# A chunked attention and MLP kernel: first weight quarter by tiles, weights loaded ahead of the rest of keys and queries

## The chip, the cores and the metric

One core of one Trainium2 chip. The metric is the device time of one execution in microseconds (us). All runs quoted are "fast": none lies more than 1.5% above the fastest of its kernel. The engines are called TensorE (PE in the profile, its weight loads PEld), VectorE (DVE), ScalarE (ACT), GpSimd (POOL) and SyncE (SP).

## The reference

Four batches, eight heads, 768 positions, head size 64. Each chunk of 32 queries looks at its own positions, 16 before, 8 behind and 8 memory positions. The result goes through a normalisation and a two-layer MLP of width 2048 with a residual.

```python
for c in range(S // 32):
    ctx = positions max(0, 32*c - 16) .. min(S, 32*c + 40)
    scores = q_c @ concat(mem_k, k[ctx]).T / sqrt(64)
    out_c  = softmax(scores) @ concat(mem_v, v[ctx])
x  = out as (4, 768, 512)
xn = (x - mean(x)) / sqrt(var(x) + 1e-6) * g_ln
out = x + relu(xn @ w_ch1) @ w_ch2          # 512 -> 2048 -> 512
```

## The kernel before

The 24 tiles of 128 tokens are worked off in eight units of three. A unit has 28 steps: 16 up steps (`up`, one for each 128 of the 2048 hidden values) and 12 down steps. Between them, a plan `at(step, ...)` places the attention of the next unit, the turns (transposes) of keys and queries, the clears of buffers and the loads. Unit 0 has nothing before it, so its own attention stands in a start stage, where filler matmuls (`stay_busy`) on a zero tile keep TensorE occupied.

Names in the profile lines: `kraw` and `qraw` are keys and queries as loaded, `KT` and `QZ` the same turned, `V` the values, `xs`, `xn` and `xT` a tile before the norm, after it and turned, `rT` the hidden values after relu, `w1c` and `w2c` the quarters of W1 and W2. `mm` and `att` are buffers in PSUM, where matmuls leave their results; a buffer is free again once another engine has copied it out.

```python
def up(u, n, hc):                      # one step: 4 matmuls of 384 columns, then relu
    p = slot("mm")[:, 0 : 128 * n]     # four PSUM banks "mm", taken in rotation
    for dt in range(4):
        nc.tensor.matmul(out=p, lhsT=free(w, i, [[4, 128]]), rhs=xT[u % 2][:, dt, 0 : 128 * n], ...)
    if hc % 2: nc.scalar.activation(out=o, in_=p, func=ACTF.Relu)
    else:      nc.vector.tensor_scalar(out=o, in0=p, scalar1=0.0, ..., op0=ALU.max)
# ... cut: start stage, loads by GpSimd in program order:
#     k, q rows 0-63 | V groups 0-5 | W1 quarters 0-2 | k, q rows 64-95 | W1 quarter 3 | W2 0, 1 | ...
    def attend(steps, kind="dma"):
        for i, (s0, s1, s2, s3) in enumerate(steps):
            t = following[i]
            at(s0, scores, t // 6, t % 6)
            at(s1, values, t // 6, t % 6)
            at(s2, norm, t % 6, t % 9)             # VectorE
            at(s3, turn_x, u + 1, i, t % 6, kind)  # TensorE turns, ScalarE copies to xT
            at(min(s3 + 3, 27), root, t % 6, t % 9)# ScalarE squares
    if u == 0:
        at(1, clear_q, 1, 0);  at(5, clear_q, 1, 1)
        at(14, clear_k, 1);    at(16, clear_v, 1)  # VectorE memsets for batch 1
        for j in (0, 2):
            at(10 + j, kq_block, 0, j, 6, NG, "att")   # turns of the rest of k and q
            at(11 + j, keep_rest)
        # ... cut
        attend(((16, 19, 19, 22), (17, 21, 21, 24), (19, 23, 23, 26)), "att")
```

The softmax here doesn't subtract the row's maximum and nothing guards it: scores larger than these inputs give would overflow.

Of the kernel before, what the change touches and what calls it, by code (L numbers as in the profile page):

```python
# [15 lines left out]
def kernel(  # L16
# [12 lines left out]
    nc = tc.nc  # L29
# [3 lines left out]
    NG = 12  # L33
    KR = 96
    HD = 80
    CUT = 64

    ctx.enter_context(tc.manual_schedule())
    sb = ctx.enter_context(tc.tile_pool(name="sb", bufs=1))
# [44 lines left out]
    def slot(kind):  # L84
        lst = {"att": att, "mm": mm}[kind]
        turn[kind] = (turn[kind] + 1) % len(lst)
        return lst[turn[kind]]
# [53 lines left out]
    def load_w1(c):  # L141
        nc.gpsimd.dma_start(
            out=w1c[c], in_=dram(moe_w_ch1, 512 * c, [[FF, 128], [128 * FF, 4], [1, 512]])
        )
# [221 lines left out]



    def up(u, n, hc):
        p = slot("mm")[:, 0 : 128 * n]  # L370
        c, i = hc // 4, hc % 4
        for dt in range(4):
            w = w1c[c][:, dt, :]
            nc.tensor.matmul(  # L374
                out=p, lhsT=free(w, i, [[4, 128]]), rhs=xT[u % 2][:, dt, 0 : 128 * n],
                start=(dt == 0), stop=(dt == 3),
            )
        o = rT[hc][:, 0 : 128 * n]
        if hc % 2:
            nc.scalar.activation(out=o, in_=p, func=ACTF.Relu)  # L380
        else:
            nc.vector.tensor_scalar(out=o, in0=p, scalar1=0.0, scalar2=None, op0=ALU.max)  # L382
# [71 lines left out]
    nc.vector.memset(busy, 0.0)  # L454
    nc.vector.memset(counts, 1.0)  # L455
    nc.vector.memset(ones32, 1.0)
    nc.vector.memset(memv16[:, :, :, 64:HD], 1.0)
    nc.sync.dma_start(out=memk32, in_=dram(mem_k, 0, [[64, 128], [128 * 64, 2], [1, 64]]))
    nc.sync.dma_start(out=g_one, in_=dram(moe_g_ln, 0, [[0, 1], [1, 512]]))
    nc.sync.dma_start(out=memv32, in_=dram(mem_v, 0, [[64, 8], [512, H], [1, 64]]))  # L460
    for h in (0, 4):
        for which in range(2):
            load_kq(0, which, 0, CUT, h, h + 4)
    keep(counts[:, 0:1], counts[:, 0:1], 16, 0.0)
    keep(counts[:, 1:2], counts[:, 1:2], -80, 0.0)
    make_identity(nc, identity)
# [19 lines left out]
    nc.gpsimd.tensor_tensor(out=band[:, 0:1], in0=band[:, 0:1], in1=zero2[:, 1:2], op=ALU.add)  # L486
    for g in range(4, 6):
        load_v_group(0, g)
    for c in range(3):
        load_w1(c)  # L490
    load_kq(0, 0, CUT, 96)
    load_kq(0, 1, CUT, 96)
    load_w1(3)
    load_w2(0)
    load_w2(1)
    for g in range(6, 8):
        load_v_group(0, g)
    load_w2(2)
    for g in range(8, NG):
        load_v_group(0, g)  # L500
    load_w2(3)
    nc.gpsimd.dma_start(
# [2 lines left out]
    )  # L505

    vec, act = nc.vector.tensor_copy, nc.scalar.copy
    first_k = [as16(slot("mm")[:, :]) for j in range(4)]
    first = slot("att")
    first_q = [as16(first[:, 0, :]), as16(first[:, 1, :])]  # L510
    for j in range(2):
        turn_kq(first_k[j], k16[0], j, CUT)
    for j in range(2):
        turn_kq(first_q[j], q16[0], j, CUT)
    for j in range(2):
        keep_k(first_k[j], 0, j, CUT, 0, 7)
        for par in range(2):
            keep_q(act, first_q[j], 0, j, par, CUT, 0, 6)
    spare = att[(turn["att"] + 1) % 2][:, 0, :]
    stay_busy(3, spare)  # L520
    first_q += first_k[0:2]
    for j in range(2, 4):
        turn_kq(first_k[j], k16[0], j, CUT)
    stay_busy(5, spare)
    for j in range(2, 4):
        turn_kq(first_q[j], q16[0], j, CUT)
    for j in range(2, 4):
        keep_k(first_k[j], 0, j, CUT, 0, 7, act if j == 2 else vec)
    for j in range(2, 4):
        for par in range(2):  # L530
            keep_q(act if j == 2 else vec, first_q[j], 0, j, par, CUT, 0, 6)
    nc.vector.memset(mhalf, -0.5)
    stay_busy(3, spare)
    scores(0, 0)
    scores(0, 1)
    stay_busy(2)
    pg = slot("mm")[:, :]
    nc.tensor.matmul(out=pg, lhsT=ones32, rhs=g_one, start=True, stop=True)
    nc.vector.tensor_copy(out=g_row, in_=pg)
    stay_busy(1)  # L540
    values(0, 0)
    norm(0, 0)
    scores(0, 2)
    stay_busy(1)
    values(0, 1)
    norm(1, 1)
    stay_busy(4)
    values(0, 2)
    norm(2, 2)
    stay_busy(2)  # L550
    turn_x(0, 0, 0, "mm")
    stay_busy(2)
    turn_x(0, 1, 1, "mm")
    stay_busy(5)
    turn_x(0, 2, 2, "mm")
    stay_busy(3)
    for t in range(3):
        root(t, t)


    units = [[t, t + 1, t + 2] for t in range(0, 6 * B, 3)]
    for u, tiles in enumerate(units):
        n = len(tiles)
        following = units[u + 1] if u + 1 < len(units) else []
        plan = {}

        def at(step, fn, *args):
            plan.setdefault(step, []).append((fn, args))
# [7 lines that stand above are left out]
                at(s2, norm, t % 6, t % 9)  # L576
                at(s3, turn_x, u + 1, i, t % 6, kind)
                at(min(s3 + 3, 27), root, t % 6, t % 9)

        def cross(steps, b, t0, t1, t2):  # L580

            for half in range(2):
                at(steps[half], cross_k, b, half, t0, t1)
                at(steps[2 + half], cross_q, half, t2 - 3, t2)

        def spread(step, b, t0, t1):
            for half in range(2):
                at(step + half, spread_q, b, half, t0, t1)

        if u == 0:  # L590
            at(1, clear_q, 1, 0)
            at(5, clear_q, 1, 1)
            at(14, clear_k, 1)
            at(16, clear_v, 1)
            for j in (0, 2):
                at(10 + j, kq_block, 0, j, 6, NG, "att")
                at(11 + j, keep_rest)
            for h in (0, 4):
                for which in range(2):
                    at(12, load_kq, 1, which, 0, 96, h, h + 4)  # L600
            for g in range(6):
                at(16, load_v_group, 1, g)
            attend(((16, 19, 19, 22), (17, 21, 21, 24), (19, 23, 23, 26)), "att")
            at(26, mem_cols, 1)
            at(26, v_mem, 1)
        elif u == 1:
            for j in (0, 2):
                at(5 + 3 * j, kq_block, 1, j, 0, NG, "att")
                at(7 + 3 * j, keep_rest)
            for g in range(6, NG):  # L610
                at(0, load_v_group, 1, g)
            for t in range(6):
                for which in range(2):
                    at(14, load_tokens, 2, which, t)
            attend(((16, 19, 19, 22), (17, 19, 20, 23), (21, 23, 23, 26)), "att")
        elif following:
            if u in (2, 4):
                attend(((2, 7, 7, 7), (4, 7, 8, 8), (9, 13, 13, 13)))
            else:
                attend(((9, 14, 14, 14), (11, 14, 15, 15), (16, 20, 20, 20)))  # L620
            if u == 2:
                cross((0, 0, 1, 1), 2, 0, 4, 3)
                at(8, mem_cols, 2)
                at(8, k_around, 2, 0, 4)
                for h in range(H):
                    at(8, load_v_head, 2, h)
                spread(9, 2, 0, 3)
                cross((14, 14, 15, 15), 2, 4, 6, 6)
            elif u == 3:
                at(1, v_mem, 2)  # L630
                at(1, v_around, 2)
                at(4, k_around, 2, 4, 6)
                spread(5, 2, 3, 6)
                for t in range(6):
                    for which in range(2):
                        at(24, load_tokens, 3, which, t)
            elif u == 4:
                for h in range(H):
                    at(0, load_v_head, 3, h)
                cross((14, 14, 15, 15), 3, 0, 4, 3)  # L640
                at(17, mem_cols, 3)
                at(17, v_mem, 3)
                at(17, v_around, 3)
                at(22, k_around, 3, 0, 4)
                spread(23, 3, 0, 3)
                cross((20, 21, 24, 25), 3, 4, 6, 6)
            elif u == 5:
                at(2, k_around, 3, 4, 6)
                spread(3, 3, 3, 6)
        for step in range(16 + 4 * n):  # L650
            if step < 16:
                up(u, n, step)
            else:
                i, part = divmod(step - 16, 4)
                if u == 0:
                    d = step - 16
                    i, part = divmod(d, 2) if d < 6 else (d % 3, d // 3)
                if following or i < n - 1:
                    down(tiles[i], i, part)
                elif part == 0:  # L660
                    down_last(tiles[i], i)
            for fn, args in plan.get(step, ()):
                fn(*args)
# [30 lines left out]
```

## Time and profile before

| | before |
|---|---|
| time, median of 3 runs (a fourth was timed later, beside the change) | 220.41 us (220.31 to 220.75) |
| profiled span | 218.5 us |
| TensorE busy | 97% of the span |
| first real W1 matmul | 22.60 us |
| first full step after W1's first quarter (22.60 + 16 x 0.1625) | 25.2 us |
| first matmul of unit 1 | 50.40 us |

A busy share includes the fillers; 97% is not 97% of useful work. From 22.6 us on TensorE does useful work almost without a gap (the largest up to unit 1 is 0.20 us), so a gain has to show as an earlier start of unit 1. The lines are in the prediction below.

### The profile page before, as it was taken

How to read it: one execution, taken by the hardware profiler on the slowest of the kernel's cores; microseconds unless marked ns; L12 is line 12 of the kernel's file. 1: busy time of each engine (PE TensorE's matmuls, PEld its weight loads, DVE VectorE, ACT ScalarE, POOL GpSimd, SP SyncE). 2: the span in 40 equal slices, each digit the busy share in tenths (PEclk: the TensorE clock that was granted, in tenths of full speed). 3: DMA queues.
4: the chain of work that ended last, by engine and by line, in shares of the span. 5: the costliest groups of instructions: out<-in, count | busy, mean ns of one | idle time of the engine just before them, and what ended most of it. 6: DMA issues, size and time to landing. Idle time of an engine off the chain costs nothing.

```text
span 218.5 us, 4954 instructions
## 1 busy us (share of the span) xinstructions
PE 212.8 (97%) x1975; PEld 129.2 (59%) x1975; DVE 118.7 (54%) x269; ACT 98.6 (45%) x196; POOL 105.0 (48%) x177
## 2 busy tenths in 40 slices
PE   7998999999999999999999999999999999999994
PEld 2554677556775577545764577446754676457553
DVE  6948566576764836823366339515386337534222
ACT  4464747635884766600555077202751165403200
POOL 7984435957995226986002999626174000300000
PEclk9999999999999999999999999999999999999999
DMA  4999999999999329995605799996743200330012
GB/s 74 181 146 206 208 202 170 192 204 193 178 145 150 105 91 128 163 139 178 87 2 99 106 176 156 162 183 96 174 122 99 96 0 11 88 103 21 0 48 96
DMA packets 93089, 27.20 MB, mean 124 GB/s; under 512 B 83673, under 2 KB 89561, under 8 KB 93018
## 3 DMA queue, kind: packets, MB, share of 16 engines
q0 software_dynamic: 67504, 14.23, 73.9%
q1 hardware_dynamic: 25562, 12.66, 24.7%
q8 instruction: 15, 0.25, 0.5%
q14 instruction: 8, 0.07, 0.1%
HBM read 28.48 MB, written 6.29 MB: 159 GB/s over the span
## 4 chain that ended last, share of the span: by engine, by line
PE 90%; DVE 3%; DMA 3%; ACT 1%; issue 1%; POOL 1%; DVEq 0%; POOLq 0%
PE mm L374 38%; PE mm L391 37%; PE att L288 5%; PE att L308 3%; DMA kraw<-in_k_dram 3%; PE att L178 2%; PE mm L409 2%; DVE xs L319 1%; ACT QZ L203 1%; DVE xn L328 1%; PE att L351 1%; PE mm L178 1%; PE att L365 1%; DVE QZ L203 1%; PE mm L365 0%
## 5 line engine op out<-in xcount | busy, mean ns | idle before, releaser
L374 PE MATMUL mm<-xT,w1c 128*128 128x384 f16 x512 | 88.5, 327 | 0.0
L391 PE MATMUL mm<-w2c,rT 128*128 128x512 f16 x368 | 84.2, 379 | 0.0
L374 PEld LDWEIGHTS <-w1c 128*128 128x128 f16 x512 | 56.8, 114 | 24.3 <-issue 0.3
L380 ACT ACTIVATE rT<-mm 128x384 f16<-128x384 f32 x64 | 31.2, 489 | 68.4 <-PE mm L374 46.8
L391 PEld LDWEIGHTS <-rT 128*128 128x128 f16 x368 | 34.8, 98 | 37.8
L382 DVE TENSOR_SCALAR rT<-mm 128x384 f16<-128x384 f32 x64 | 35.1, 554 | 35.9 <-PE mm L374 35.8
L398 DVE SCALAR_TENSOR_TENSOR osb<-mm,rstd,xs 128x512 f32<-128x512 f32 x23 | 17.3, 751 | 42.3 <-PE mm L391 29.9
L295 ACT ACTIVATE AT<-att,band 96x512 f16<-96x512 f32 x48 | 30.1, 678 | 10.9 <-PE att L288 10.6
L337 POOL TENSOR_SCALAR veps<-squares 128x1 f32<-128x1 f32 x24 | 4.6, 191 | 50.5 <-ACT junk L334 49.2
L116 POOL DMA_DIRECT2D V<-in_v_dram x24 | 21.5, 903 | 8.5 <-DMA w1c<-in_moe_w_ch_dram 4.3
L334 ACT ACTIVATE junk<-xs,nmean 128x512 f16<-128x512 f32 x24 | 17.3, 719 | 7.1 <-DVE nmean L325 6.7
L328 DVE SCALAR_TENSOR_TENSOR xn<-xs,nmean,g_row 128x512 f16<-128x512 f32 x24 | 18.5, 771 | 0.9
L319 DVE SCALAR_TENSOR_TENSOR xs<-att,rec 128x512 f32<-128x512 f32 x24 | 16.6, 692 | 0.8
L276 POOL COPY QZ<-kraw 64x768 f16<-64x768 f16 x16 | 14.4, 900 | 3.5 <-DMA kraw<-qraw 2.9
L203 ACT COPY QZ<-att 64x384 f16<-64x384 f16 (+1 forms) x20 | 12.0, 599 | 8.4 <-PE att L178 8.2
L288 PE MATMUL att<-QZ,KT 128*128 128x128 f16 x192 | 14.8, 219 | 0.2 <-DVE QZ L203 0.2
L288 PEld LDWEIGHTS <-KT 128*128 128x128 f16 x192 | 12.6, 98 | 4.0 <-issue 0.3
L341 POOL TENSOR_TENSOR rstd<-veps,mhalf 128x1 f32<-128x1 f32 x24 | 13.3, 552 | 2.0
L365 PE MATMUL mm<-busy 128*128 128x512 f16 x34 | 11.1, 454 | 1.2 <-DVE counts L455 1.2
L122 POOL DMA_DIRECT2D V<-in_v_dram x16 | 12.0, 807 | 0.0
L268 POOL COPY KT<-KT 128x128 f16<-128x128 f16 (+4 forms) x16 | 4.2, 293 | 15.6 <-DMA KT<-kraw 15.6
L241 POOL DMA_DIRECT2D kraw<-in_k_dram x12 | 11.4, 954 | 0.0
(68 smaller groups left out, 133.9 us busy)
## 6 DMA issues: line engine op xcount, KB each, us to landing
out_dram<-osb SPq DMA_DIRECT2D x23, 256.0 KB, 3.0
w1c<-in_moe_w_ch_dram POOLq DMA_DIRECT2D x4, 512.0 KB, 10.0
w2c<-in_moe_w_ch_dram POOLq DMA_DIRECT2D x4, 512.0 KB, 14.2
V<-in_v_dram POOLq DMA_DIRECT2D x20, 88.0 KB, 8.5
kraw<-in_k_dram POOLq DMA_DIRECT2D x12, 128.0 KB, 4.5
qraw<-in_q_dram POOLq DMA_DIRECT2D x12, 128.0 KB, 4.6
V<-in_v_dram POOLq DMA_DIRECT2D x16, 96.0 KB, 5.3
kraw<-in_k_dram POOLq DMA_DIRECT2D x3, 256.0 KB, 6.2
```

The lines of the kernel that those rows point to most:

```text
L116: nc.gpsimd.dma_start(out=V[b % 2][r : r + hi - lo, g, :, 0:64], in_=dram(v, b * H * HS + lo * D, [[64, hi - lo], [HS, H], [1, 64]]),)
L203: copy(out=free(QZ[b % 2][rows, g0, j, par, :], 0, [[512, g1 - g0], [8, 8], [1, 8]]), in_=free(pv[rows, :], 8 * g0, [[8, g1 - g0], [1, 8], ...
L288: nc.tensor.matmul(out=p[:, gg, 128 * j : 128 * j + 128], lhsT=KT[b % 2][:, (4 * g + j) * KR : (4 * g + j) * KR + 128], rhs=QZ[b % 2][:, g ...
L295: nc.scalar.activation(out=free(a, 32 * c, [[512, 2], [64, 8], [1, 32]], KR), in_=free(p, 32 * c, [[512, 2], [64, 8], [1, 32]], KR), func= ...
L319: nc.vector.scalar_tensor_tensor(out=x.rearrange("p (h d) -> p h d", h=H), in0=free(p, 0, [[128, H], [1, 64]]), scalar=1.0, in1=free(r, 0, ...
L328: nc.vector.scalar_tensor_tensor(out=xn[i], in0=x, scalar=nmean[i], in1=g_row, op0=ALU.add, op1=ALU.mult,)
L334: nc.scalar.activation(out=junk, in_=xs[xi], func=ACTF.Square, bias=nmean[i], accum_out=squares[i],)
L374: nc.tensor.matmul(out=p, lhsT=free(w, i, [[4, 128]]), rhs=xT[u % 2][:, dt, 0 : 128 * n], start=(dt == 0), stop=(dt == 3),)
L380: nc.scalar.activation(out=o, in_=p, func=ACTF.Relu)
L382: nc.vector.tensor_scalar(out=o, in0=p, scalar1=0.0, scalar2=None, op0=ALU.max)
L391: nc.tensor.matmul(out=p, lhsT=rT[hc][:, 128 * i : 128 * i + 128], rhs=w2c[hc // 4][:, hc % 4, :], start=(hc == 0), stop=(hc == 15),)
L398: nc.vector.scalar_tensor_tensor(out=o, in0=p, scalar=rstd[t % 9], in1=xs[t % 9], op0=ALU.mult, op1=ALU.add,)
```

## The change

The intent: start unit 0's up projection before its third tile is ready, by doing W1's first quarter for tiles 0 and 1 together and for tile 2 behind; have all of W1 there in time, by loading it ahead of the rest of keys and queries; and so turn that rest behind the up projection, not inside it.

```diff
-    CUT = 64
+    CUT = (64, 48)                     # rows of k and q loaded first
@@ loads
-    for c in range(3):
+    for c in range(4):
         load_w1(c)
-    load_kq(0, 0, CUT, 96)
-    load_kq(0, 1, CUT, 96)
-    load_w1(3)
+    for which in range(2):
+        load_kq(0, which, CUT[which], 96)
     load_w2(0)
     load_w2(1)
-    for g in range(6, 8):
+    for g in range(6, 10):
         load_v_group(0, g)
     load_w2(2)
-    for g in range(8, NG):
+    for g in range(10, NG):
         load_v_group(0, g)
@@ start stage (cut: q copies in two parts, fillers moved, squares of tiles 0 to 2 moved to unit 0)
+    nc.tensor.matmul(out=banks[2], lhsT=ones32, rhs=g_one, start=True, stop=True)
+    nc.vector.tensor_copy(out=g_row, in_=banks[2])
     scores(0, 0)
     scores(0, 1)
-    # (the same broadcast of g stood here)
@@ unit 0
-            at(1, clear_q, 1, 0)
-            at(5, clear_q, 1, 1)
-            at(14, clear_k, 1)
-            at(16, clear_v, 1)
+            at(5, clear_q, 1, 0)
+            at(8, clear_q, 1, 1)
+            at(11, clear_v, 1)
+            at(13, clear_k, 1)
             for j in (0, 2):
-                at(10 + j, kq_block, 0, j, 6, NG, "att")
-                at(11 + j, keep_rest)
+                at(15, kq_block, 0, j, 6, NG, "mm")
+                at(15, keep_rest)
+            for t in range(3):
+                at(11 + t, root, t, t)
             for h in (0, 4):
                 for which in range(2):
-                    at(12, load_kq, 1, which, 0, 96, h, h + 4)
+                    at(15, load_kq, 1, which, 0, 96, h, h + 4)
-            attend(((16, 19, 19, 22), (17, 21, 21, 24), (19, 23, 23, 26)), "att")
+            attend(((18, 21, 21, 24), (19, 23, 23, 26), (22, 25, 25, 27)), "att")
@@ steps 0 to 3 of unit 0
+                for hc in range(4):
+                    up(0, 2, hc)                    # tiles 0 and 1, 256 columns
+                    if hc == 2:
+                        turn_x(0, 2, 2, "mm")
+                for hc in range(4):
+                    up(0, 3, hc, 2)                 # tile 2, 128 columns
```

More of the change, by code (lines that the diff above doesn't have):

```diff
@@ L365, in stay_busy, with up @@
             nc.tensor.matmul(out=p, lhsT=busy[:, 0:128], rhs=busy, start=True, stop=True)
-    def up(u, n, hc):
-        p = slot("mm")[:, 0 : 128 * n]
+    def up(u, n, hc, t0=0):
+        lo, hi = 128 * t0, 128 * n
+        p = slot("mm")[:, 0 : hi - lo]
         c, i = hc // 4, hc % 4
@@ L374, in up @@
             nc.tensor.matmul(
-                out=p, lhsT=free(w, i, [[4, 128]]), rhs=xT[u % 2][:, dt, 0 : 128 * n],
+                out=p, lhsT=free(w, i, [[4, 128]]), rhs=xT[u % 2][:, dt, lo:hi],
                 start=(dt == 0), stop=(dt == 3),
             )
-        o = rT[hc][:, 0 : 128 * n]
+        o = rT[hc][:, lo:hi]
         if hc % 2:
@@ L456 @@
     nc.vector.memset(ones32, 1.0)
+    nc.vector.memset(mhalf, -0.5)
     nc.vector.memset(memv16[:, :, :, 64:HD], 1.0)
@@ L462 @@
         for which in range(2):
-            load_kq(0, which, 0, CUT, h, h + 4)
+            load_kq(0, which, 0, CUT[which], h, h + 4)
     keep(counts[:, 0:1], counts[:, 0:1], 16, 0.0)
@@ L507 @@
     vec, act = nc.vector.tensor_copy, nc.scalar.copy
-    first_k = [as16(slot("mm")[:, :]) for j in range(4)]
+    banks = [slot("mm")[:, :] for j in range(4)]
+    first_k = [as16(p) for p in banks]
     first = slot("att")
-    first_q = [as16(first[:, 0, :]), as16(first[:, 1, :])]
+    first_q = [as16(first[:, i, :]) for i in range(2)] + first_k[0:2]
+    spare = att[(turn["att"] + 1) % 2][:, 0, :]
     for j in range(2):
-        turn_kq(first_k[j], k16[0], j, CUT)
+        turn_kq(first_k[j], k16[0], j, CUT[0])
@@ L513 @@
     for j in range(2):
-        turn_kq(first_q[j], q16[0], j, CUT)
+        turn_kq(first_q[j], q16[0], j, CUT[1])
     for j in range(2):
-        keep_k(first_k[j], 0, j, CUT, 0, 7)
+        keep_k(first_k[j], 0, j, CUT[0], 0, 7)
         for par in range(2):
-            keep_q(act, first_q[j], 0, j, par, CUT, 0, 6)
-    spare = att[(turn["att"] + 1) % 2][:, 0, :]
+            keep_q(act, first_q[j], 0, j, par, CUT[1], 0, 6)
     stay_busy(3, spare)
-    first_q += first_k[0:2]
     for j in range(2, 4):
-        turn_kq(first_k[j], k16[0], j, CUT)
@@ L524 @@
-    stay_busy(5, spare)
+        turn_kq(first_k[j], k16[0], j, CUT[0])
     for j in range(2, 4):
-        turn_kq(first_q[j], q16[0], j, CUT)
+        keep_k(first_k[j], 0, j, CUT[0], 0, 7, act if j == 2 else vec)
+    stay_busy(4, spare)
     for j in range(2, 4):
-        keep_k(first_k[j], 0, j, CUT, 0, 7, act if j == 2 else vec)
-    for j in range(2, 4):
-        for par in range(2):
-            keep_q(act if j == 2 else vec, first_q[j], 0, j, par, CUT, 0, 6)
-    nc.vector.memset(mhalf, -0.5)
@@ L533 @@
-    stay_busy(3, spare)
+        turn_kq(first_q[j], q16[0], j, CUT[1])
+    for g0, g1 in ((0, 2), (2, 6)):
+        for j in range(2, 4):
+            for par in range(2):
+                keep_q(act if j == 2 else vec, first_q[j], 0, j, par, CUT[1], g0, g1)
+    nc.tensor.matmul(out=banks[2], lhsT=ones32, rhs=g_one, start=True, stop=True)
+    nc.vector.tensor_copy(out=g_row, in_=banks[2])
     scores(0, 0)
     scores(0, 1)
-    stay_busy(2)
-    pg = slot("mm")[:, :]
-    nc.tensor.matmul(out=pg, lhsT=ones32, rhs=g_one, start=True, stop=True)
@@ L539 @@
-    nc.vector.tensor_copy(out=g_row, in_=pg)
-    stay_busy(1)
+    stay_busy(3)
     values(0, 0)
     norm(0, 0)
+    stay_busy(3)
     scores(0, 2)
-    stay_busy(1)
     values(0, 1)
     norm(1, 1)
-    stay_busy(4)
+    stay_busy(1)
+    turn_x(0, 0, 0, "mm")
+    stay_busy(3)
     values(0, 2)
     norm(2, 2)
-    stay_busy(2)
-    turn_x(0, 0, 0, "mm")
-    stay_busy(2)
+    stay_busy(3)
     turn_x(0, 1, 1, "mm")
-    stay_busy(5)
-    turn_x(0, 2, 2, "mm")
-    stay_busy(3)
-    for t in range(3):
-        root(t, t)
+    stay_busy(4)
@@ L650 @@
         for step in range(16 + 4 * n):
-            if step < 16:
+            if u == 0 and step == 0:
+                for hc in range(4):
[4 more added lines that the diff above has]
+                    up(0, 3, hc, 2)
+            elif u == 0 and step < 4:
+                pass
+            elif step < 16:
                 up(u, n, step)
```

## The prediction

> **What bounds the kernel now.** I read the page first, then busy time by stage, then the chain of waits for the first 45 us, then each engine's instructions in order of time.
>
> ```profile
> PE 212.8 (97%) x1975; PEld 129.2 (59%) x1975; DVE 118.7 (54%) x269; ACT 98.6 (45%) x196; POOL 105.0 (48%) x177
> ...
> PE 90%; DVE 3%; DMA 3%; ACT 1%; issue 1%; POOL 1%; DVEq 0%; POOLq 0%
> ```
>
> TensorE is busy 97% of the span and 90% of the chain. But 34 + 11 of its matmuls are fillers on a zero tile, all before 22.6 us, so only the start has anything to give. By stage (columns: PE, PEld, DVE, ACT, POOL busy, granted clock, DMA, GB/s):
>
> ```profile
> 0.00:10.00 10.00, 8.54 (x119) 3.92 (x120) 7.92 (x21) 4.07 (x7) 8.57 (x23) 1.00 0.90 124
> 10.00:22.60 12.60, 11.68 (x147) 6.17 (x145) 7.95 (x22) 7.16 (x15) 8.45 (x12) 1.00 1.70 177
> 22.60:36.60 14.00, 13.80 (x193) 10.03 (x193) 9.20 (x18) 8.73 (x21) 5.72 (x9) 1.00 1.28 200
> 36.60:50.40 13.80, 13.80 (x134) 7.46 (x133) 9.37 (x27) 7.25 (x14) 10.64 (x17) 1.00 1.46 186
> ```
>
> From 22.6 us (up projection of unit 0) and from 36.6 us (its down projection) TensorE is full. Unit 1 begins at 50.4, and everything behind it stays as it is. So my question is one number: **when does unit 1 start?** In the start stage the chain of waits (start, length, what) is VectorE's three norms in a row:
>
> ```profile
> 15.90 0.22 DVE rec L318
> ...
> 17.07 0.75 DVE xn L328
> 17.82 0.13 DVE rec L318
> ...
> 20.72 0.76 DVE xn L328
> 21.48 0.05 issue
> 21.53 0.40 PE mm L351 x4
> 21.92 0.65 PE mm L365 x3
> 22.57 0.03 issue
> 22.60 7.31 PE mm L374 x44
> ```
>
> One norm is 1.83 to 1.91 us. The last tile is turned at 21.53, copied, and the first real matmul is at 22.60. Tiles 0 and 1 were turned at 19.06 and 19.71 and only waited.
>
> **What the Trainium skill says.** "TensorE: Matmul & The Clock Gate", section "Back-to-back issue gap", gives N/2.4 + 2.5 ns warm, but some 81 ns for 128 columns in a real stream with weight loads. The trace agrees with the first at 384 columns (44 matmuls in 7.31 us less the drain, 162 ns each), and the scores' 128 columns take 56 ns (8 in 0.45 us); for the strided w1c weights (load 114 ns, not 98) at 128 columns no row exists, so I take 56 to 81. "PSUM — Partial Sum Buffer", section "Engine vs sequencer instructions", calls the ScalarE and VectorE queues strict FIFOs; the trace shows it (VectorE's relus stand behind memsets). That decides two steps below. "DMA: Bandwidth & Descriptors", section "Two DMAs through the same engine are not ordered", says that descriptors of one queue start in order but may complete in another; here the large POOL transfers land in issue order: W1 quarters at 18.45, 20.95, 23.8 and 28.55 (issue plus 7.2, 8.9, 11.0, 13.6).
>
> **Part by part.**
>
> (a) Smaller first q. Rows 64 to 48 takes 2 x 64 KB out of the front. At 194 to 197 GB/s (6 to 9 us in the DMA view of the first 60 us) that is 0.33 us for the second k half (lands at 8.96 now, so about 8.63) and 0.66 us for all that follows: second q 10.56 to 9.9, W1's first quarter 18.45 to 17.8.
>
> (b) The chain to the norms. Second q turned at 10.2 to 10.85 instead of 10.82 to 11.5. The q copies are cut into groups 0-2 and 2-6: a 384-wide piece is 0.555 us on VectorE and 0.473 on ScalarE, so a 128-wide one about 0.29 and 0.26 (taking off the elements at one per cycle, an estimate). The first pieces are done by 11.53; the fp32 broadcast of g (1.06 us) now fills exactly that time on TensorE, and scores start at 11.9, not at 12.1 to 12.7. Before, this broadcast stood between scores and values, and VectorE waited for its copy until 15.13. Now: exp 12.6 to 13.8, values at 13.9, first norm at about 14.4 against 15.90. The norms run back to back: xn at 16.3, 18.2, 20.0 (now 17.8, 19.6, 21.5). V groups land at 10.9 to 16.3 now and sooner after, so they don't hold this.
>
> (c) First W1 quarter by tiles. Tile 1's copy ends near 19.35. Twelve matmuls of 256 columns at 109 ns (256/2.4 + 2.5) run 19.45 to 20.75, the turn of tile 2 follows, four more to 21.4, the copy of tile 2 ends near 21.8, then 16 of 128 columns, 0.9 to 1.3 us. Step 4 begins at **22.95** (22.75 to 23.15); before it began at 22.60 + 16 x 0.1625 = 25.2. Gain 2.2 us, of which some 1.5 by (a) and (b), 0.7 by doing it by tiles.
>
> (d) The up projection. Steps 4 to 15 are 12 x 0.65 = 7.8 us. W1's quarters 1, 2, 3 come at 20.3, 23.15, 25.8 (the fourth ahead of the rest of k and q), needed at 22.95, 25.5, 28.1: no wait. The rest of k and q lands at about 27 and 29, before step 15 ends at 30.75.
>
> (e) A new wait for PSUM. All four memset groups of the next batch now lie within steps 5 to 13 on VectorE, which also does every second relu. In the trace before:
>
> ```profile
> 24.45 1.34 DVE L431 MEMSET QZ<- 64x1536 uint32 x1 [0.38 <-issue]
> 25.82 1.02 DVE L382 TENSOR_SCALAR rT<-mm 128x384 f16<-128x384 f32 x2
> ...
> 36.78 0.27 DVE L435 MEMSET V<- 32x256 uint32 x1
> 37.16 0.27 DVE L436 MEMSET V<- 32x256 uint32 x1
> 37.81 1.34 DVE L437 MEMSET V<- 128x1536 f16 x1 [0.38 <-issue]
> ```
>
> A clear of QZ costs 1.34 + 0.38; the V group runs from 36.78 to 39.49, 2.7 us, and was in the down stage. From step 4's start X: relus 4, 6, 8, 10, two QZ clears and V's: relu 12 ends near X + 9.8 (V's clear starts at X + 6.5). The turns of q now use the four mm banks in rotation, so the first of them needs the bank of step 12. TensorE gets there at X + 7.8 + 0.74 (k turned) = X + 8.55: a stall of about **1.3 us**. The turns are 4 x 0.74 = 2.97 us. So step 16 is at X + 12.05 = 35.0 (36.6 before; the old stage had 0.6 us of waits of its own, which go).
>
> (f) The down stage. The same work: 12 x 0.865 + 3 scores at 0.45 + 3 values at 0.375 + two turns at 0.22 = 13.3 us, to 48.3. W2's third quarter lands near 39.5 and is wanted at 41.4; its fourth 42.6 against 45.
>
> (g) A new wait at the end of unit 0. The last values now stand at step 25 and the last turn after step 27, the last one, with no matmul behind it. Counted from the start of step 21: values end at 6.12; VectorE first does the output of tile 0 (ready 5.74, 0.75), then the norm to 8.56; the turn at 8.6, where TensorE was free at 8.07. On ScalarE two squares of roots (0.85 each in the trace: 22.44, 23.29, 24.14) are queued ahead of the copy: copy of tile 1 to 7.9, squares to 9.6, copy of the last tile to 10.2. Unit 1's first matmul is at 10.25, **1.95 us** of idle TensorE (2.18 with the turn in it).
>
> **Sum.** Unit 1 at 48.3 + 2.2 = 50.5 against 50.4 now. In terms of the changes: 2.2 gained at X, 0.6 of old waits gone, 1.3 new in (e), 1.95 new in (g), 0.3 rounding and turn: within 0.5 us of nothing. Behind that nothing changes. Both stalls are counted whole though, and an earlier or shorter VectorE queue would take from each, while little can make them longer; so I put the point 0.5 us under the old time: **219.9 us**.
>
> **Rivals.** (1) The head start is kept: no bank is waited for and the last turn hides. The full share of TensorE in the stage and the harmless old memsets speak for it; the FIFO count in (e) and step 27 against it. Without (e) 218.6, without both about 216.8. (2) DMA becomes the bound of unit 0: it moves about 200 GB/s to 40 us with all engines busy, and the margins for W2 in (f) are 2 us, 0.7 for its second quarter. Four V groups now go ahead of the third quarter. If that slips by 2 us, 220.5 to 221.5. (3) The first quarter by tiles gains nothing, since 128-column matmuls wait for strided weights and the copy of tile 2 waits behind relus on ScalarE: X = 23.8, and with both stalls 221.2.
>
> **Range and chances.** Errors of half a microsecond in X, of 0.6 in (e) and 0.5 in (g) add in squares to 0.9, so eight times in ten within 1.3: **218.6 to 221.2**. Faster than 216.0 needs all of the head start and no new wait: **0.03**. Slower than 224.8: **0.02**. Same: **0.95**.
>
> **What would show it.** (a) second k half lands near 8.6. (b) first norm starts near 14.4 with no wait for the g broadcast. (c) first real matmul near 19.45, first full 384-column one near 22.95. (e) TensorE idle before the mm turns of q, released by a VectorE relu. (g) TensorE idle of about 2 us before unit 1's first matmul, released by the ScalarE copy to xT, with two squares ahead of it. I am wrong if both idles are missing (time under 218), or if idle before w2c matmuls is released by a DMA (time over 221).

## The result and the profile after

| | before | after |
|---|---|---|
| time, median | 220.52 us (4 runs, 220.31 to 220.75) | 220.25 us (4 runs, 219.88 to 220.56) |
| first real W1 matmul | 22.60 | 20.20 |
| first full step after the first quarter | 25.2 | 23.46 (22.57 + 16 x 0.056) |
| first matmul of unit 1 | 50.40 | 50.62 |

The ratio is 0.9987, with a 95% interval of 0.9967 to 1.0007: the same. The step start comes from the trace: 16 matmuls of 128 columns and 48 of 384 stand in one row of 8.86 us; less the end of the last, which overlaps what follows (0.17), and 48 x 0.1625 us, 0.89 us is left for the 16.

The page after, the lines of the engines and of the chain that ended last:

```profile
PE 211.7 (97%) x1984; PEld 129.5 (59%) x1984; DVE 119.0 (54%) x273; ACT 98.9 (45%) x200; POOL 104.9 (48%) x177
...
PE 73%; DVE 2%; ACT 0%; issue 0%; DVEq 0%
```

The engines' line looks the same. The chain's shares add up to some 75%, not 100%. In order of time that chain begins only at 50.10 us, with the ScalarE copy ahead of unit 1. So 73% is no smaller part of TensorE than 90%, it is a shorter chain. By stage, with the columns as in the prediction:

```profile
0.00:10.00 10.00, 8.75 (x118) 3.93 (x119) 7.87 (x21) 3.52 (x6) 8.54 (x23) 1.00 1.04 124
10.00:22.60 12.60, 11.97 (x156) 7.39 (x157) 9.09 (x25) 8.33 (x19) 8.49 (x12) 1.00 1.72 165
22.60:36.60 14.00, 13.41 (x200) 9.89 (x200) 10.73 (x26) 8.79 (x22) 4.62 (x6) 1.00 1.40 195
36.60:50.40 13.80, 12.53 (x126) 6.64 (x124) 7.50 (x19) 7.44 (x15) 11.88 (x20) 1.00 1.28 189
```

TensorE had 0.2 us idle in the third stage and none in the fourth. Now it has 0.59 and 1.27, and the last idle stretch runs on to 50.62. TensorE's instructions in order of time (start, length, engine, line, what, and in brackets the idle before it and what ended it) show where:

```profile
20.20 1.47 PE L376 MATMUL mm<-xT,w1c 128*128 128x256 f16 x12
22.57 8.86 PE L376 MATMUL mm<-xT,w1c 128*128 128x128 f16 x64 [0.24 <-ACT xT L356]
...
32.81 0.87 PE L178 MATMUL mm<-identity,qraw 96*64 96x96 f16 x32 [0.59 <-DVE rT L384]
...
49.05 0.40 PE L351 MATMUL att<-identity,xn 128*128 128x128 f16 x4 [0.31 <-DVE xn L328]
50.62 4.06 PE L376 MATMUL mm<-xT,w1c 128*128 128x384 f16 x24 [1.18 <-ACT xT L356]
```

Real work begins 2.4 us sooner, full steps 1.7. Then 0.59 us go while a VectorE relu is awaited, 0.31 us for the last norm and 1.18 us for the last copy to xT. What VectorE and ScalarE did there, each in order of time (VectorE first):

```profile
29.65 0.27 DVE L437 MEMSET V<- 32x256 uint32 x1
...
30.68 1.34 DVE L439 MEMSET V<- 128x1536 f16 x1 [0.38 <-issue]
32.06 0.26 DVE L442 COPY V<-counts 128x8 f16<-128x8 f16 x2
32.21 0.55 DVE L384 TENSOR_SCALAR rT<-mm 128x384 f16<-128x384 f32 x1
```

```profile
48.39 0.72 ACT L334 ACTIVATE junk<-xs,nmean 128x512 f16<-128x512 f32 x1
...
49.29 0.72 ACT L334 ACTIVATE junk<-xs,nmean 128x512 f16<-128x512 f32 x1
49.91 0.19 ACT L334 ACTIVATION_READ_ACCUMULATOR junk<-xs,nmean 128x1 f32 x1
50.01 0.56 ACT L356 COPY xT<-att 128x512 f16<-128x512 f16 x1
```

The relu of step 12 stands behind the clear of V. The last copy stands behind two squares, although its turn had run at 49.05.

### The profile page after: what moved, and what is told of

Read it like the earlier page. It is cut to its first block, busy times and chain, and to the rows that moved or that the text cites. A ratio compares the mean times of both kernels' runs of the same rounds, so it can differ in the third digit from the quotient of the medians.

```text
span 218.9 us, 4983 instructions
## 1 busy us (share of the span) xinstructions
PE 211.7 (97%) x1984; PEld 129.5 (59%) x1984; DVE 119.0 (54%) x273; ACT 98.9 (45%) x200; POOL 104.9 (48%) x177
## 4 chain that ended last, share of the span: by engine, by line
PE 73%; DVE 2%; ACT 0%; issue 0%; DVEq 0%
PE mm L376 32%; PE mm L393 32%; PE att L288 4%; PE att L308 2%; PE mm L411 2%; PE att L178 1%; DVE xn L328 1%; DVE xs L319 1%; DVE rT L384 0%; PE att L351 0%; ACT xT L356 0%; DVE osb L416 0%; DVE rec L318 0%; DVE KT L168 0%; DVE nmean L325 0%
## 5 line engine op out<-in xcount | busy, mean ns | idle before, releaser
L376 PE MATMUL mm<-xT,w1c 128*128 128x384 f16 (+2 forms) x528 | 88.5, 322 | 1.5 <-ACT xT L356 1.4
L376 PEld LDWEIGHTS <-w1c 128*128 128x128 f16 x528 | 57.8, 114 | 24.9 <-issue 1.7
L382 ACT ACTIVATE rT<-mm 128x384 f16<-128x384 f32 (+2 forms) x66 | 31.5, 478 | 72.0 <-PE mm L376 49.4
L384 DVE TENSOR_SCALAR rT<-mm 128x384 f16<-128x384 f32 (+2 forms) x66 | 35.5, 541 | 34.1 <-PE mm L376 33.7
L276 POOL COPY QZ<-kraw 64x768 f16<-64x768 f16 x16 | 14.4, 900 | 3.3 <-DMA kraw<-qraw 2.7
L308 PEld LDWEIGHTS <-AT 96*64 96x64 f16 x384 | 7.5, 111 | 6.5 <-ACT AT L295 2.1
L241 POOL DMA_DIRECT2D qraw<-in_q_dram x12 | 11.0, 918 | 0.4 <-PE att L288 0.4
```

Of the source, the lines that this page charges most:

```text
L276: nc.gpsimd.tensor_copy(out=QZ[b % 2][rows, 6 * half + t0 : 6 * half + t1, :, par, :], in_=QT[rows, (24 * half + 4 * t0) * 64 : (24 * half ...
L384: nc.vector.tensor_scalar(out=o, in0=p, scalar1=0.0, scalar2=None, op0=ALU.max)
```

## The experiments

Each was timed in five rounds beside the kernel before. Besides the time I give the **stretch from the first W1 matmul to unit 1**, read from TensorE's instructions in order of time. It leaves out what happens in the first microseconds, which varies from run to run. In the profile of the changed kernel it is 50.62 - 20.20 = 30.42 us. From unit 1's first matmul to the end, all thirteen profiles take 168.09 to 168.23 us, so what happens before unit 1 decides the time. An idle time in brackets counts from the modelled end of the matmul before it; by the starts of the matmuls a wait costs some 0.2 us more.

### 1. The changed kernel again

No edit.

> The changed kernel itself, once more on this chip, as the base for the other three. Expected 220.2 us, within 0.3 us of the kernel before. Its second profile also shows whether the four fillers ahead of the first turns take 1.61 us again (as in its first profile) or 1.04 us (as in the profile of the kernel before): if it is luck of the clock's warm-up, they vary from run to run of the same kernel.

Measured: 220.29 us (219.72 to 220.83), ratio 1.000 (0.9982 to 1.0017). The stretch is 49.92 - 19.50 = 30.42 us again, but it began 0.70 us sooner. The fillers ahead of the first turns, in the changed kernel's first profile and then in this one:

```profile
5.88 1.61 PE L365 MATMUL mm<-busy 128*128 128x512 f16 x4
```

```profile
5.75 1.04 PE L365 MATMUL mm<-busy 128*128 128x512 f16 x4
```

The same four fillers took 1.61 and 1.04 us. In the slow case their weight loads start 0.41 and 0.43 us apart, about twice the usual 0.216. So it is luck of the clock's warm-up. The granted clock column of that stretch reads 1.00 in both, but only because the view counts a stretch without a record as 1.00: the trace's first record of the full clock stands at 7.06 us in the slow case and at 5.44 in the fast one. Over the twelve profiles that have such a record it stands at 3.91 to 7.06, and with the same four fillers the first turns come the later, the later it stands (6.04 to 7.41). The Trainium skill, "TensorE: Matmul & The Clock Gate", Part 1, says that the activity window runs free and the transition varies from run to run; this agrees, though its +-500 ns is far less than the 3.15 us seen here. What follows: single runs of one kernel differ by 0.7 us and more, so 0.3 us in a median is little evidence, and the stretch is the better measure.

### 2. Only the front of the change

```diff
 # on top of the changed kernel: loads, kq_block and attend as before
-            at(15, kq_block, 0, j, 6, NG, "mm")
+            at(10 + j, kq_block, 0, j, 6, NG, "att")
-            attend(((18, 21, 21, 24), (19, 23, 23, 26), (22, 25, 25, 27)), "att")
+            attend(((16, 19, 19, 22), (17, 21, 21, 24), (19, 23, 23, 26)), "att")
 # clears at steps 4, 6, 14, 16; squares of tiles 0-2 at 5, 6, 7; W1's last quarter behind the rest of k, q;
 # loads of the next batch's k and q at step 12 again
```

> Only the front of the change: the smaller first q, the split q copies, the broadcast of g moved, the first W1 quarter by tiles. The order of the loads behind it, the turns of the rest of keys and queries (after steps 10 and 12) and the attention steps are those of the kernel before. Theory (the front gains, two new waits in unit 0 eat it): the real work starts 1.8 us earlier and no new wait follows, so unit 1 starts near 48.5 us and the time is about 218.4. Rival (the front itself gains nothing that lasts, since DMA bounds unit 0): unit 1 starts at 50 or later with idle time of TensorE before w1c or w2c matmuls released by a DMA, and the time stays at 220.

Measured: 218.48 us (218.31 to 219.30), ratio 0.9927 (0.9911 to 0.9944). The stretch is 48.94 - 20.47 = 28.47 us, 1.95 shorter than the change's, with no wait for a DMA in it. The front is real, and what the change lost it lost behind the front. (The profiled run, 218.85 us, is a late one: its granted clock fell to 0.50 from 11.6 to 15.0 us.)

### 3. The clears of K and V behind the turns

```diff
-            at(11, clear_v, 1)
-            at(13, clear_k, 1)
+            at(16, clear_k, 1)
+            at(16, clear_v, 1)
```

> The changed kernel with the clears of K and V moved back to step 16, behind the turns. Theory: relu 12 no longer stands behind the V clear, the 0.6 to 0.7 us of TensorE idle before the turns of q goes, and since the end of unit 0 waits on work that all shifts with TensorE, the time falls by the same 0.6 to 219.6. Rival (the bank wait is harmless, another wait takes its place): the idle before the q turns goes, but W2's second or third quarter or the ScalarE copies of q are waited for, and the time stays within 0.2 us of the changed kernel.

Measured: 219.85 us (219.35 to 220.62), ratio 0.9986 (0.9967 to 1.0005); stretch 49.84 - 19.62 = 30.22 us. The idle before the q turns is gone, which shows its cause. But in TensorE's instructions a new one stands in its place:

```profile
35.07 1.89 PE L393 MATMUL mm<-w2c,rT 128*128 128x512 f16 x8 [0.41 <-DMA w2c<-in_moe_w_ch_dram]
```

The second quarter of W2 landed at 35.0 us in this run. My theory for this run and its rival were both half right. From the first full step to the first down step it takes 10.74 us, 0.77 less than in experiment 1; from there to unit 1 it takes 16.22, 0.57 more, the wait for W2. The time alone is unclear. Two of the six runs (220.29 and 220.62) had a mean granted clock of 0.992; the other four have a median of 219.65.

### 4. The last turn one step earlier

```diff
-attend(((18, 21, 21, 24), (19, 23, 23, 26), (22, 25, 25, 27)), "att")
+attend(((18, 20, 20, 23), (19, 22, 22, 25), (21, 24, 24, 26)), "att")
```

> The changed kernel with the attention of the next unit moved up by one step where the rotation of the banks allows, so that the last turn follows step 26 and not 27. Theory: the idle of about 1.5 us (2.05 from the end of the last down matmul to unit 1) shrinks to 0.2 or 0.3 before the turn, and the time falls by 1.7 to 218.5. Rival (the chain of norms on VectorE is the bound there, not the place of the turn): the wait moves to the last turn, which waits for its norm, and the gain is under 0.7.

Measured: 218.83 us (218.59 to 218.92), ratio 0.9936 (0.9922 to 0.9949); stretch 48.89 - 20.07 = 28.82 us, 1.60 shorter. The end of unit 0, in TensorE's order:

```profile
46.70 1.03 PE L393 MATMUL mm<-w2c,rT 128*128 128x512 f16 x4
47.79 0.40 PE L351 MATMUL att<-identity,xn 128*128 128x128 f16 x4
48.03 1.03 PE L393 MATMUL mm<-w2c,rT 128*128 128x512 f16 x4
48.89 2.28 PE L376 MATMUL mm<-xT,w1c 128*128 128x384 f16 x13
```

The last down step now runs while the copy is made, and unit 1 follows it without a gap. The turn hardly waits for its norm. Since values, norm and turn all moved by one step, what bound the end was their place in the plan, not the speed of the norms.

### 5. Both repairs

> Both repairs together: the clears behind the turns and the attention one step earlier. Alone they gave 0.44 and 1.46 us by the medians. Theory (two separate waits): they add, 218.4. Rival (behind the bank wait stands the second quarter of W2, which TensorE waited 0.41 us for once the bank wait was gone): this DMA wait takes most of the first gain back, and the time is that of the earlier turn alone, 218.6 to 218.8.

The edits of 3 and 4 together. Measured: 217.75 us (4 runs, 217.41 to 218.04), ratio 0.9885 (0.9868 to 0.9901); stretch 48.13 - 20.08 = 28.05 us, 2.37 shorter than the change's. This is the fastest kernel by its median, and better than the 218.4 I expected. In the trace the two waits simply add: 2.37 is the 1.60 of experiment 4 and the 0.77 that the bank wait had cost (experiment 3). The two medians alone summed to less because experiment 3 gave most of its gain back to W2. No wait for W2 appears: its second quarter landed at 34.5 us and was wanted at 34.07 + 0.86 = 34.93. In experiment 3 it landed 0.5 later and was wanted 0.4 sooner, since the profiled run had begun sooner. This wait comes and goes with the start and with the transfers; its margin is 0.4 us.

### 6. The front, with the first quarter whole

```diff
-                for hc in range(4):
-                    up(0, 2, hc)
-                    if hc == 2:
-                        turn_x(0, 2, 2, "mm")
-                for hc in range(4):
-                    up(0, 3, hc, 2)
+                turn_x(0, 2, 2, "mm")
+                for hc in range(4):
+                    up(0, 3, hc)
```

> The front alone, but its first W1 quarter whole: the turn of tile 2 first, then 16 matmuls of 384 columns. Prediction's step (c): doing it by tiles is worth 0.7 us, the rest of the front 1.5. From the profile of the changed kernel: the turn could come at about 20.8 instead of 21.5, the copy ends 0.7 sooner, then 16 x 0.1625 = 2.6 us instead of 0.85, so full steps begin 1.0 us later, which gives 219.3 to 219.5. Rival (tiles gain nothing that lasts): 218.5 as with tiles.

Measured: 218.88 us (218.59 to 219.39), ratio 0.9940 (0.9924 to 0.9956), against 0.9927 with tiles; the intervals overlap. It is neither the 219.3 to 219.5 that I expected nor the rival's 218.5. From TensorE's order:

```profile
20.64 0.40 PE L351 MATMUL mm<-identity,xn 128*128 128x128 f16 x4 [0.40 <-DVE xn L328]
21.71 7.31 PE L376 MATMUL mm<-xT,w1c 128*128 128x384 f16 x44 [0.67 <-ACT xT L356]
```

Full steps begin at 21.71 + 2.60 = 24.31 us, and unit 1 at 49.52. The profile of experiment 8, the front with tiles, began its first turns at the same moment (7.27 against 7.29) and reached unit 1 at 48.53. At equal starts the tiles gain 1.0 us in the trace; by the medians, in different jobs, 0.4. The lower figure may come from the luck of the warm-up; how much of it stays open.

### 7. The front, with the q turns in the mm banks

```diff
-                at(10 + j, kq_block, 0, j, 6, NG, "att")
+                at(10 + j, kq_block, 0, j, 6, NG, "mm")
```

> The front alone with the old places of the turns of the rest of keys and queries, but their q halves in the mm banks, as the change has it. The old stage has about 0.6 us in which TensorE waits for the att banks between the two halves (0.20 by the profile before the second q turns, the rest around). Theory: this goes and the VectorE queue there is short enough, so 218.0 to 218.2. Rival: the mm banks make the next up steps wait for the ScalarE copies of q, and the time is 218.5 or more.

Measured: 218.32 us (217.71 to 218.97), ratio 0.9908 (0.9889 to 0.9928). The intervals overlap with experiment 2, and the stretch, 48.63 - 19.95 = 28.68 us, is no shorter than its 28.47. The wait before the second q turns went, but nothing of it reached unit 1. Two other waits took its place. W1's last quarter landed at 30.26 us in this run, about 1 us later than in experiment 2, and the weights of step 12 waited for it, as TensorE's weight loads show:

```profile
30.30 0.47 PEld L376 LDWEIGHTS <-w1c 128*128 128x128 f16 x4 [0.40 <-DMA w1c<-in_moe_w_ch_dram]
```

And the first down matmul, whose bank the last q turn had used, came at 34.83, just after the ScalarE copy of that bank had ended at 34.77: the rival's wait. Inconclusive in time; the theory's gain is not there in the trace.

### 8. The front, with 64 rows of q

```diff
-    CUT = (64, 48)
+    CUT = (64, 64)
```

> The front alone with the first part of q at 64 rows again, so the one piece of the front that touches the first transfers is undone. Prediction's step (a): second k half 0.33 us later, second q half and all behind it 0.66 us later. Measured landings with 48 rows: second k half 8.3 to 8.9, second q half 9.5 to 9.8; with 64 rows in the profile of before 9.0 and 10.6. TensorE turned the second q at 10.2 (clock warm early) to 10.9 (late), so the later q should cost 0 to 0.5: 218.5 to 219.0. Rival (everything behind follows the transfers): 219.1 or more.

Measured: 218.39 us (218.01 to 218.41, 5 runs), ratio 0.9904 (0.9887 to 0.9920). Undoing the smaller q costs nothing that shows; the time is under both ranges. The second halves of k and q landed at 8.5 and 9.8 us with 64 rows; with 48 rows, over eleven profiles, at 8.3 to 9.0 and 9.5 to 9.9. TensorE turned the second q only at 10.74, 1.0 us after it had landed, so its landing held nothing. The later landings in the profile of before (9.0 and 10.6) are not repaired by fewer rows; why they were later there isn't settled.

### 9. The copy ahead of the squares

```diff
-                at(min(s3 + 3, 27), root, t % 6, t % 9)
+                if u != 0:
+                    at(min(s3 + 3, 27), root, t % 6, t % 9)
+            if u == 0:                     # behind the last turn
+                for t in following:
+                    at(27, root, t % 6, t % 9)
```

> The changed kernel with only the order on ScalarE at the end of unit 0 altered: the copy of the last tile before the three squares of the roots, not behind two of them. The last turn ran at 49.05 and its copy only began at 50.01. Theory (two causes at the end, the late norm and the squares queued ahead): the copy begins at 49.5, unit 1 0.55 us sooner, 219.7. Rival (only the late norm counts): no change. Second rival (only the queue counts): over 1.2 us gained.

Measured: 219.71 us (219.60 to 220.36), ratio 0.9979 (0.9964 to 0.9994); stretch 49.81 - 19.90 = 29.91 us, 0.51 shorter. In TensorE's order the idle before unit 1 is 0.67 instead of 1.18 us:

```profile
48.74 0.40 PE L351 MATMUL att<-identity,xn 128*128 128x128 f16 x4 [0.31 <-DVE xn L328]
49.81 4.06 PE L376 MATMUL mm<-xT,w1c 128*128 128x384 f16 x24 [0.67 <-ACT xT L356]
```

So the wait at the end has two causes, as foreseen: 0.5 us are the squares, and about 1.1 more (the 1.60 of experiment 4 less this 0.51) is that a norm, a turn and a copy have no matmul beside them.

### 10. The changed kernel with the old order of loads

```diff
-    for c in range(4):
+    for c in range(3):
         load_w1(c)
     # the rest of k and q, then
+    load_w1(3)
     # W2 0 and 1, then
-    for g in range(6, 10):
+    for g in range(6, 8):
         load_v_group(0, g)
     # W2 2, then
-    for g in range(10, NG):
+    for g in range(8, NG):
         load_v_group(0, g)
```

> The changed kernel with the loads in the old order: the rest of keys and queries before W1's last quarter. The last quarter then lands at about 28.6 to 29.6 (as in the runs with the old order) and is wanted at 28.1 to 28.6. Theory (the new order is needed once the up projection runs through): a wait of 0.3 to 1.0 us before step 12, part of which the bank wait behind it swallows, so 220.3 to 220.8. Rival (the order doesn't matter): no DMA wait, 220.2.

Measured: 220.48 us (220.30 to 221.00), ratio 1.0008 (0.9991 to 1.0024); stretch 50.72 - 19.93 = 30.79 us. W1's last quarter came too late:

```profile
29.51 2.79 PE L376 MATMUL mm<-xT,w1c 128*128 128x384 f16 x16 [0.95 <-DMA w1c<-in_moe_w_ch_dram]
```

The bank wait of 0.59 us is gone in this run: relu 12 ended at 32.49 us, while TensorE was still turning k (from 32.23). The net loss in the stretch is 0.37 us; the median alone, 220.48 against 220.29, would not show it. By the trace, an up projection that runs through needs the new order. The old places of the turns, in the middle of it, hid the late quarter (experiment 7 apart).

### 11. Both repairs and fewer fillers

```diff
     mem_cols(0)
-    stay_busy(4)
+    stay_busy(1)
```

> Both waits gone, and one filler instead of four ahead of the first turns. In some profiles these four took 1.04 us, in others up to 1.61, and the start of everything behind shifted by it. Theory (they hold TensorE past the landing of the first k while the clock is slow): the first turns start 0.6 to 1.2 us sooner, the second k half (8.3 to 8.9) is then the bound, and the median falls by 0.2 to 0.4 to 217.4, with less spread. Rival (they warm the clock): without them the clock comes up later, matmuls behind run at half rate, and the time is 217.8 or more.

Measured: 218.47 us (217.44 to 220.15), ratio 0.9925 (0.9894 to 0.9956). My expectation failed. The profiled run was among the fastest seen, 217.44 us, with the first turns at 6.04; but other runs took up to 220.15, a spread of 2.7 us where experiment 5 has 0.6. The rival fits: the three slowest runs (218.53, 218.93 and 220.15) have a mean granted clock of 0.992, 0.991 and 0.984, the other three 1.0. Where in the run the clock was low is not shown, as only a fast one was profiled. The three undisturbed runs have a median of 217.76, no better than experiment 5. The same mark stands in four more kernels: each of the ten runs with a mean clock below 0.995 is slower than every other run of its kernel.

## Why the prediction was right

The time, 220.25 us, is 0.35 from the point and inside the range, and the mechanism held: a head start of about two microseconds, taken back by two new waits in the same unit. The parts, in us:

| | predicted | the change, two profiles | before | both repairs |
|---|---|---|---|---|
| X, first full step | 22.95 | 23.46, 22.76 | 25.2 | 23.34 |
| X to the first down matmul (bank wait inside) | 12.05 | 11.52, 11.51 | 11.40 | 10.73 |
| from there to unit 1 (wait at the end inside) | 15.5 | 15.64, 15.65 | 13.81 | 14.06 |
| first matmul of unit 1 | 50.5 | 50.62, 49.92 | 50.40 | 48.13 |

- **(a), smaller first q: its effect was wrong.** The transfers behind it did not come sooner: W1's first quarter landed at 17.8 to 19.2 us in the eleven profiles with 48 rows (17.8 predicted) and at 17.9 and 18.4 in the two with 64, and experiment 8 shows no cost of undoing it. The sum survived because the chain in (b) hung on TensorE's and VectorE's order, not on the rows.
- **(b), first norm near 14.4 us: right.** It started at 14.44 in the second profile and at 15.13 in the first, whose fillers ran at half rate. I had not reckoned with that luck. The 128-wide copies took 0.28 to 0.30 and 0.26 us, as estimated.
- **(c), full steps from 22.95: right within the luck of the start.** They came at 22.76 (21.87 + 0.89) and 23.46, the latter outside my 22.75 to 23.15. The 128-column matmuls took 56 ns, the low end of what I allowed. The share of the tiles in it, 0.7, lies between the two values that the runs give.
- **(d), no wait for W1: right**, and experiment 10 shows it is the new order that does it.
- **(e), a stall of 1.3 us for a bank: the mechanism right, the size too large.** By experiment 5 the wait cost 11.52 - 10.73 = 0.79 us. TensorE arrived about as reckoned, but V's clear began at X + 6.2 and not X + 6.5, and relu 12 ended at 32.76, X + 9.3 and not X + 9.8: relus and clears took less than I summed. The old stage's own waits, 0.6 by my count, were 11.40 - 10.73 = 0.67.
- **(f), W2 in time: right for the change.** In its first profile the margins were 1.2 us for the second quarter (0.7 reckoned), 1.6 for the third (1.9) and 1.5 for the fourth (2.4). Without the bank wait the second's was used up once (experiment 3).
- **(g), 1.95 us at the end of unit 0, 2.18 with the turn: right.** From the end of the last down matmul, about 48.57, to unit 1 at 50.62 is 2.05 us. Experiments 4 and 9 confirm both its parts.
- **Sum: right, with some luck.** In the first profile X was 0.5 late and the stall 0.5 short, which cancelled. The recount in terms of the changes was wrong: 2.2 + 0.6 against 1.3 + 1.95 + 0.3 is a loss of 0.75 us, not "within 0.5 us of nothing". The half microsecond taken off the sum at the end was a guess; the sum itself, 220.5, was no farther from the result than the point.

Whether a few tenths of gain remain is not settled. With the fillers fast in both, the change reached unit 1 0.48 us sooner (49.92 against 50.40), but the medians differ by 0.27 us in one job and 0.01 in the other.

Of the rivals, the kept head start is refuted for the change as it is, but describes experiment 5: 216.8 was said without both waits, 217.75 was reached. Without (e) alone 218.6 was said and 219.85 was reached (experiment 3), since (e) was smaller and W2 took its place. DMA as the bound is refuted for the change and comes near once the bank wait is gone. Tiles that gain nothing are refuted by the trace.

## What to carry to other kernels

Follow a head start to the next point where everything meets, here the first matmul of the next unit, and count what each engine's queue now holds on the way: two waits of 0.8 and 1.6 us, behind engines half idle on average, ate a front worth 1.8 us and the 0.7 us that moving the turns had saved. Where a stage ends, leave the last producer a step of other work behind it. And where the same kernel starts its work at different moments from run to run (19.50 and 20.20 us here), compare stretches within the traces, not only medians.

## What the Trainium skill lacked or had wrong

- "TensorE: Matmul & The Clock Gate", section "Back-to-back issue gap", gives some 81 ns for 128 columns in a real stream with weight loads. Here 16 such matmuls with strided weights took 0.89 us, 56 ns each, the page's figure for the isolated case.
- The same page, Part 1, has the run-to-run luck of the warm-up. It gives +-500 ns for it in one place and 6 to 14 slow matmuls of one kernel in another; here the first record of the full clock stands at 3.91 to 7.06 us in twelve profiles, which at 0.43 us a filler from 1.25 us on is 6 to 14 fillers and fits the second, not the first. It does not say what that does further on: in two profiles of the changed kernel everything behind shifted by 0.70 us, with the same stretch of 30.42 us.
- "DMA: Bandwidth & Descriptors" has nothing on how landings vary between runs: W1's first quarter landed at 17.8 and at 18.8 us in two profiles of the same kernel, and a first q of 64 rows landed no later than one of 48 (9.8 against 9.5 to 9.9 us).
